# Denominators of phi for batches 0 and 1 from nine whole-array products of the exponentials, in a tile of their own

## The chip, the cores and the metric

The kernel runs on one core of a Trainium2 chip, in one launch. The metric is the device time of that launch in microseconds (us). A core has a matrix engine (TensorE, PE in the profile; its weight loads are listed apart as PEld), VectorE (DVE), ScalarE (ACT), GpSimd (POOL) and SyncE (SP), which here only issues DMAs. Each engine takes its instructions in order and waits for the others through semaphores. SBUF is the working memory of 128 partitions, PSUM the banks that TensorE writes to.

## The reference

Attention through 32 memories per head, then a gated feed-forward block with a product over the sequence (8 batches, 8 heads, 576 rows, 64 columns):

```
a = exp(phi - max(phi, over rows));  a = a / (sum(a, over rows) + 1e-9)
k_m = a^T k;  v_m = a^T v                              # 32 memories per head
attn = softmax(q k_m^T / 8);  x = attn v_m             # heads side by side: 576 x 512
h = relu(x w_in);  u, v = halves of h
v_n = (v - mean) / sqrt(var + 1e-6)
out = (u * (w_spatial v_n + b_spatial)) w_out
```

The change concerns `sum(a, over rows)`: one sum for each head and memory, 256 per batch.

## The kernel before, in words

Every batch goes through nine kinds of steps, each a generator that issues a few instructions and yields: P (`memory_weights`), K (`memories`), Q (`queries`), S (`scores`), M (`products`), V (`gate`), U (`units`), G (`spatial`), O (`project`). The weights have steps of their own: D, E and L load and decode w_in, X does w_out, W loads the spatial weights, T transposes them, B does the bias; Z is a warm-up product that nothing reads. Three written lists of letters say which step comes when: START (batch 0 from the beginning, batches 1 and 2 as far as they run ahead), PLAN (once per batch) and LAST. A quote mark means one batch ahead. Each engine's queue, SP's too, holds its instructions exactly in that order. The change does not touch the lists.

P loads the batch's phi into `phi_sb`, which has one buffer: 128 partitions are 2 heads x 64 groups of rows, and along a partition lie 4 head pairs j, 9 rows i of a group and 32 memories m. Step 1 issues the DMA (line 297). Steps 2 to 5 take the maximum over the 9 rows in four DVE operations (`over_rows`, lines 286 to 292), 6 to 9 take it across partitions (transpose, reduce, copy, transpose), 10 subtracts it on DVE (line 316), 11 is the exponential on ACT, in place (line 323), and 12 to 15 are the same four DVE operations with add: the sums over the 9 rows, tile `es`.

K loads k and v (steps 1 and 2). Steps 3 and 4 multiply the exponentials with k and v: 72 products in 64x32 pieces of the array (line 342; five values of i in step 3, four in step 4), and step 4 ends with eight small products that sum `es` over the 64 partitions of a head (line 354), into spare columns of the same two PSUM banks. Step 5 adds 1e-9 and takes the reciprocal on DVE (lines 364, 365: `den`). Steps 6 to 8 are copies on ACT that multiply by it (lines 369, 378), 9 and 10 transposes, 11 and 12 copies to `kT` and `vT`, from which S and M take their operands.

The part of START around the steps in question:

```
Q Z Q*3 Z P Q P*4 K Q P Q*2 P*2 K P Z P*6 K D1*2 K Z E0 K*3 D1 K Q*2 K D1 E1 E0 E1 P' Z K*2 W D0
...
V0 T1 P' L0 V2 V0 V2 L1 T3 T1 V0 P' V0 M0 B M0 P'*2 V0 V2 K' T1 M0*2 T4 K' P'' V0 K'*2 V0 T4 U2
```

So in batch 0 steps P 10 to 15 follow each other, and K 3 (the first of line 342) comes right behind. In batch 1 step P 12 stands between the first gate block's products (V0, line 621) and those of block V2, P 13 behind V0's statistics, P 14 and 15 behind M0's first step, and K 4 (second half of line 342 and line 354) two steps later. Batch 1's phi load (first P') is followed on SP's queue by W (spatial weights, lines 239 to 242) and D0 (w_in).

There is one pool of four single PSUM banks (`bank`) and one of two double ones (`banks`). A bank comes free when the last instruction that reads it is done. In START's last quoted line the two kvm banks of K', and one each for V0 and V2, are in use together; M0 takes two when they come free.

A float32 product appears in the trace as two weight loads and two matmuls.

Of the kernel before, what the change touches and what calls it, by code (L numbers as in the profile page):

```python
# [10 lines left out]
F32 = mybir.dt.float32  # L11
# [3 lines left out]
AF = mybir.ActivationFunctionType  # L15
ALU = mybir.AluOpType
# [39 lines left out]
def memory_attention_spatial_gate(  # L56
# [29 lines left out]
    nc = tc.nc  # L86
    B, H, S, D = q.shape
    MEM = phi.shape[3]
    DM = H * D
    DFF = w_in.shape[1]  # L90
    P = 128
# [3 lines left out]
    NJ = H // 2  # L95
    HALF = S // 2
    NB = S // 32
    NX = HALF // 32
    SCALE = 1.0 / math.sqrt(D)

    const = ctx.enter_context(tc.tile_pool(name="const", bufs=1))
    one = ctx.enter_context(tc.tile_pool(name="one", bufs=1))
# [5 lines left out]
    def bank(name):  # L108
        return ps1.tile([P, 512], F32, tag="b1", name=name)
# [11 lines left out]
    nc.scalar.activation(minus, ident, AF.Copy, scale=-1.0)  # L121

    phi_sb = const.tile([P, NJ, NX, MEM], F32, name="phi_sb")
    kv_sb = const.tile([P, NJ, 2, NX * D], F32, name="kv_sb")
    ones = const.tile([P, 2], F32, name="ones")
    nc.gpsimd.memset(ones, 1.0)
    t2 = const.tile([P, 512], F32R, name="t2")
    nc.gpsimd.memset(t2[SR:P, :].bitcast(F32), 1.0)

# [6 lines left out]
    state = {}  # L136
# [144 lines left out]
        yield  # L281


    def over_rows(to, op):
        half = one.tile([P, NJ, 4, MEM], F32, name="half")
        nc.vector.tensor_tensor(half, phi_sb[:, :, 0:4], phi_sb[:, :, 4:8], op=op)
        yield
        nc.vector.tensor_tensor(half[:, :, 0:2], half[:, :, 0:2], half[:, :, 2:4], op=op)
        yield
        nc.vector.tensor_tensor(to, half[:, :, 0], half[:, :, 1], op=op)  # L290
        yield
        nc.vector.tensor_tensor(to, to, phi_sb[:, :, 8], op=op)
        yield

    def memory_weights(b, _):

        nc.sync.dma_start(
            phi_sb.rearrange("p j i m -> p j (i m)"),
            phi[b].rearrange("(j r) (p i) m -> (r p) j (i m)", r=2, i=NX),
        )  # L300
        yield
        mx = one.tile([P, NJ, MEM], F32, name="mx")
        yield from over_rows(mx, ALU.max)
        mt = bank(f"mt_{b}")[:, 0:P]
        nc.tensor.transpose(mt, mx.rearrange("p j m -> p (j m)"), ident)
        yield
        cm = one.tile([P, 2], F32, name="cm")
        nc.vector.tensor_reduce(cm, mt.rearrange("s (r p) -> s r p", r=2), axis=AX.X, op=ALU.max)
        yield
        cmb = one.tile([P, 2, 64], F32, tag="vmn", name="cmb")  # L310
        nc.scalar.copy(cmb, cm[:, :, None].to_broadcast([P, 2, 64]))
        yield
        mb = bank(f"mb_{b}")[:, 0:P]
        nc.tensor.transpose(mb, cmb.rearrange("s r p -> s (r p)"), ident)
        yield
        nc.vector.tensor_tensor(
            phi_sb,
            phi_sb,
            mb.rearrange("p (j m) -> p j m", j=NJ)[:, :, None, :].to_broadcast([P, NJ, NX, MEM]),
            op=ALU.subtract,  # L320
        )
        yield
        nc.scalar.activation(phi_sb, phi_sb, AF.Exp)
        yield
        es = state["es", b] = one.tile([P, NJ, MEM], F32, tag="mx", name="es")
        yield from over_rows(es, ALU.add)

    def memories(b, _):
        for n, x in enumerate((k, v)):
            nc.sync.dma_start(  # L330
                kv_sb[:, :, n, :], x[b].rearrange("(j r) (p i) d -> (r p) j (i d)", r=2, i=NX)
            )
            yield

        kvb = [bank(f"kvm_{b}_{r}") for r in range(2)]
        kvm = [x[:, 0 : 2 * D].rearrange("p (n d) -> p n d", n=2) for x in kvb]
        esm = [x[:, 2 * D : 2 * D + 2] for x in kvb]
        halves = (slice(0, 64), slice(64, P))
        for i in range(NX):
            for j in range(NJ):  # L340
                for r in range(2):
                    nc.tensor.matmul(  # L342
                        kvm[r][32 * j : 32 * j + 32],
                        phi_sb[halves[r], j, i, :],
                        kv_sb[halves[r], j, :, i * D : (i + 1) * D],
                        start=(i == 0),
                        stop=(i == NX - 1),
                    )
            if i == 4:
                yield  # L350
        es = state.pop(("es", b))
        for j in range(NJ):
            for r in range(2):
                nc.tensor.matmul(
                    esm[r][32 * j : 32 * j + 32],
                    es[halves[r], j, :],
                    ones[halves[r]],
                    start=True,
                    stop=True,
                )  # L360
        yield
        den = one.tile([P, 2], F32, name="den")
        for r in range(2):
            nc.vector.tensor_scalar_add(den[:, r : r + 1], esm[r][:, 0:1], 1e-9)
        nc.vector.reciprocal(den, den)
        yield
        kmn = one.tile([P, 2, 2, D], F32, name="kmn")
        for r in range(2):
            nc.scalar.activation(
                kmn[:, r],  # L370
                kvm[r][:, 0, None, :].to_broadcast([P, 2, D]),
                AF.Copy,
                scale=den[:, r : r + 1],
            )
            yield
        vmn = one.tile([P, 2, D], F32, tag="vmn", name="vmn")
        for r in range(2):
            nc.scalar.activation(vmn[:, r], kvm[r][:, 1], AF.Copy, scale=den[:, r : r + 1])
        yield
        tk = bank(f"tk_{b}")[:, 0 : 2 * P]  # L380
        for r in range(2):
            nc.tensor.transpose(
                tk[:, r * P : (r + 1) * P], kmn[:, r].rearrange("p c d -> p (c d)"), ident
            )
        yield
        tv = bank(f"tv_{b}")[:, 0:P]
        nc.tensor.transpose(tv, vmn.rearrange("p r d -> p (r d)"), ident)
        yield
        kT = one.tile([P, 2, P], F32, name="kT")
        state["kT", b] = kT  # L390
        nc.scalar.copy(kT.rearrange("p r s -> p (r s)"), tk)
        yield
        vT = one.tile([P, P], F32, name="vT")
        state["vT", b] = vT
        nc.scalar.copy(vT, tv)
        yield
# [384 lines left out]
    def warm_up(b, _):  # L781
# [12 lines left out]
    }  # L794
    BATCH = {
        "P": memory_weights, "K": memories, "Q": queries, "S": scores, "M": products,
        "V": gate, "U": units, "G": spatial, "O": project,
    }
# [67 lines left out]
```

## Time and profile before

| | |
|---|---|
| median of 3 runs | 416.6 us (416.01 to 416.63) |
| the profiled execution | 417.52 us, of which the span from the first to the last instruction is 415.7 |
| ACT busy | 230.0 us (55%) |
| POOL busy | 46.5 us (11%) |
| weight loads (PEld) busy | 339.3 us (82%) |
| mean granted TensorE clock | 0.986 of full speed |
| DMA | 50.70 MB, mean 122 GB/s |

Busy time is the union of an engine's instructions. "Idle before, releaser" is the time that an engine stood before an instruction, and what ended it; "issue" means that the profile shows no reason. The chain of waits is followed back from the last instruction: at each step to what released it, or to the instruction before it on its engine. A granted clock of 1.00 is 2.4 GHz and 0.50 is 1.2 GHz.

### The profile page before, as it was taken

The numbers are of one execution on the slowest core, as the hardware profiler recorded it, in microseconds if no ns is written. First come the engines' busy times: TensorE is split into PE (matmuls) and PEld (weight loads), VectorE is DVE, ScalarE is ACT, GpSimd is POOL, SyncE is SP. The second block draws the span as 40 slices with busy tenths as digits, with TensorE's granted clock in tenths as the row PEclk, the third lists the DMA queues.
The fourth block names the chain that finished last, engine by engine and source line by source line (L and its number), as shares of the span: only waits on it lengthen the run. The fifth ranks groups of instructions, "written<-read, shape, count | busy, mean of one in ns | idle before, by whom it ended". The sixth has DMA issues, their size and how long they took to land.

```text
span 415.7 us, 9467 instructions
## 1 busy us (share of the span) xinstructions
PE 401.5 (97%) x3965; PEld 339.3 (82%) x3965; DVE 283.8 (68%) x540; ACT 230.0 (55%) x425; POOL 46.5 (11%) x131
## 2 busy tenths in 40 slices
PE   6789999999999999999999999999999999999996
PEld 3544788989798888978798888988798788989984
DVE  1477999986988468947888468947887368924430
ACT  2468889546644476337644476347734476348321
POOL 1000321003200210003200210003200210013000
PEclk9888999999999999999999999999999999999999
DMA  8899595035810891039500990049401510020003
GB/s 297 320 383 279 116 342 142 2 107 111 236 50 31 176 301 24 0 105 276 123 2 17 247 258 7 0 117 290 97 2 37 101 50 0 2 76 27 0 30 97
DMA packets 85790, 50.70 MB, mean 122 GB/s; under 512 B 66226, under 2 KB 70322, under 8 KB 85748
## 3 DMA queue, kind: packets, MB, share of 16 engines
q1 hardware_dynamic: 85748, 50.10, 42.0%
q8 instruction: 31, 0.51, 0.5%
q14 instruction: 11, 0.09, 0.1%
HBM read 40.65 MB, written 9.44 MB: 120 GB/s over the span
## 4 chain that ended last, share of the span: by engine, by line
PE 87%; DMA 4%; DVE 4%; ACT 3%; issue 1%; SPq 0%; ACTq 0%
PE ps L725 29%; PE po L765 22%; PE pu L687 12%; PE pv L621 10%; PE kvm L342 3%; PE mp L589 3%; PE sc L523 2%; DMA w_rem<-in_moe_w_spatial_dram 2%; DMA q_all<-in_q_dram 1%; PE idle L785 1%; PE pv L630 1%; PE pv L631 1%; DMA out_dram<-o 1%; PE tq L410 1%; PE wt L255 1%
## 5 line engine op out<-in xcount | busy, mean ns | idle before, releaser
L725 PE MATMUL ps<-wth,vh 128*128 128x288 f32 x256 | 57.1, 304 | 0.0
L725 PE MATMUL ps<-wth,vl 128*128 128x288 f32 x256 | 54.8, 296 | 0.0
L725 PE MATMUL ps<-wtl,vh 128*128 128x288 f32 x256 | 54.5, 294 | 0.0
L765 PE MATMUL po<-woh,gl 128*128 128x512 f32 x128 | 50.4, 394 | 0.0
L765 PE MATMUL po<-woh,gh 128*128 128x512 f32 x128 | 50.4, 394 | 0.0
L645 DVE BATCH_NORM_STATS2 st<-vr 128x6 f32<-128x512 f32 (+1 forms) x40 | 27.0, 675 | 34.1 <-ACT vr L626 33.3
L765 PE MATMUL po<-wol,gh 128*128 128x512 f32 x128 | 50.2, 392 | 0.0
L725 PEld LDWEIGHTS ps<-wth,vh 128*128 128x128 f32 x256 | 41.2, 190 | 8.7 <-ACT vh L663 5.0
L650 POOL TENSOR_SCALAR rs<-mv 128x1 f32<-128x1 f32 (+1 forms) x40 | 8.8, 221 | 330.4 <-DVE grl L749 153.4
L747 ACT CAST gh<-g 128x512 fp32r<-128x512 f32 x32 | 19.8, 621 | 46.4 <-DVE g L736 45.2
L771 ACT COPY o<-po 128x512 f32<-128x512 f32 x36 | 21.0, 584 | 37.3 <-PE po L765 20.0
L725 PEld LDWEIGHTS ps<-wth,vl 128*128 128x128 f32 x256 | 41.1, 188 | 0.0
L725 PEld LDWEIGHTS ps<-wtl,vh 128*128 128x128 f32 x256 | 41.1, 188 | 0.0
L736 DVE TENSOR_TENSOR g<-u,ps 128x576 f32<-128x576 f32 x32 | 23.4, 751 | 17.1 <-PE ps L725 17.1
L665 DVE TENSOR_TENSOR vl<-vr,vh 128x512 fp32r<-128x512 f32 x32 | 21.6, 681 | 18.0 <-ACT vh L663 17.8
L660 ACT ACTIVATE vr<-vr,sh,rs 128x512 f32<-128x512 f32 (+1 forms) x40 | 32.1, 816 | 3.0 <-POOL sh L655 3.0
L626 ACT ACTIVATE vr<-pv 128x512 f32<-128x512 f32 x32 | 19.2, 600 | 19.4 <-PE pv L621 13.1
L687 PE MATMUL pu<-ah,mh 128*128 128x288 f32 x128 | 28.7, 306 | 0.0
L765 PEld LDWEIGHTS po<-wol,gh 128*128 128x128 f32 x128 | 24.1, 188 | 5.2
L765 PEld LDWEIGHTS po<-woh,gl 128*128 128x128 f32 x128 | 24.1, 188 | 5.2
L765 PEld LDWEIGHTS po<-woh,gh 128*128 128x128 f32 x128 | 24.0, 188 | 5.2
L687 PE MATMUL pu<-al,mh 128*128 128x288 f32 x128 | 27.4, 296 | 0.0
(141 smaller groups left out, 861.3 us busy)
## 6 DMA issues: line engine op xcount, KB each, us to landing
kv_sb<-in_k_dram SPq DMA_DIRECT2D x8, 1152.0 KB, 7.0
kv_sb<-in_v_dram SPq DMA_DIRECT2D x8, 1152.0 KB, 7.7
out_dram<-o SPq DMA_DIRECT2D x32, 256.0 KB, 2.3
q_sb<-in_q_dram SPq DMA_DIRECT2D x28, 288.0 KB, 5.6
phi_sb<-in_phi_dram SPq DMA_DIRECT2D x8, 576.0 KB, 5.0
raw<-in_moe_w_in_dram SPq DMA_DIRECT2D x8, 512.0 KB, 10.3
raw<-in_moe_w_out_dram SPq DMA_DIRECT2D x4, 512.0 KB, 6.0
q_all<-in_q_dram SPq DMA_DIRECT2D x1, 1152.0 KB, 5.4
```

Source lines behind the costliest of these rows:

```text
L342: nc.tensor.matmul(kvm[r][32 * j : 32 * j + 32], phi_sb[halves[r], j, i, :], kv_sb[halves[r], j, :, i * D : (i + 1) * D], start=(i == 0), ...
L621: nc.tensor.matmul(pv, x[:, r, cs], m[:, r, DM:DFF], start=(n == 0), stop=(n == 5))
L626: nc.scalar.activation(vr, pv, AF.Relu)
L645: nc.vector.bn_stats(st6, vr)
L660: nc.scalar.activation(vr, vr, AF.Identity, bias=sh, scale=rs)
L665: nc.vector.tensor_tensor(vl[:, st, :], vr, vh[:, st, :].bitcast(F32), op=ALU.subtract)
L687: nc.tensor.matmul(pu[:, hf, 0:HALF], m[:, r, cs], a[:, r, hf * HALF : (hf + 1) * HALF], start=(n == 0), stop=(n == 5),)
L725: nc.tensor.matmul(ps[:, hf, 0:HALF], a, w[:, hf * HALF : (hf + 1) * HALF], start=(n == 0), stop=(n == len(ops) - 1),)
L736: nc.vector.tensor_tensor(g.rearrange("p (a s) -> p a s", a=2), u[:, dt, :].rearrange("p (a s) -> p a s", a=2), ps[:, :, 0:HALF], op=ALU.mult,
L747: nc.scalar.copy(hi, x)
L765: nc.tensor.matmul(po, a, w, start=(n == 0), stop=(n == 11))
L771: nc.scalar.copy(o, po)
```

## The change

The exponentials get a tile of their own, `phi_exp`, with rows ahead of head pairs, so that for one row i the 4 x 32 columns (j, m) lie together. For batches 0 and 1 step P 12 issues nine products, one for each i: the 128x128 block of exponentials is the stationary operand, and `side`, two columns that mark the partitions of either head, moves. They accumulate in a bank of their own and give all 256 sums. P 13 adds 1e-9 and takes the reciprocal; P 14 and 15 are empty. In K the eight small products and the denominator's operations are left out for these batches. Batches 2 to 7 keep both, reading from `phi_exp`.

```
+    phi_exp = const.tile([P, NX, NJ, MEM], F32, name="phi_exp")
...
+    side = const.tile([P, 2], F32, name="side")
+    nc.gpsimd.memset(side, 0.0)
+    for r in range(2):
+        nc.gpsimd.memset(side[64 * r : 64 * r + 64, r : r + 1], 1.0)
...
-    def over_rows(to, op):
+    def over_rows(to, x, op):
...
-        nc.scalar.activation(phi_sb, phi_sb, AF.Exp)
-        yield
+        nc.scalar.activation(phi_exp.rearrange("p i j m -> p j i m"), phi_sb, AF.Exp)
+        yield
+        if b < 2:
+            sums = bank(f"es_{b}")[:, 0:2]
+            for i in range(NX):
+                nc.tensor.matmul(
+                    sums, phi_exp[:, i].rearrange("p j m -> p (j m)"), side, start=(i == 0), stop=(i == NX - 1)
+                )
+            yield
+            den = state["den", b] = one.tile([P, 2], F32, name=f"den_{b}")
+            nc.vector.tensor_scalar_add(den, sums, 1e-9)
+            nc.vector.reciprocal(den, den)
+            yield
+            return
         es = state["es", b] = one.tile([P, NJ, MEM], F32, tag="mx", name="es")
-        yield from over_rows(es, ALU.add)
+        yield from over_rows(es, phi_exp.rearrange("p i j m -> p j i m"), ALU.add)
...
                         kvm[r][32 * j : 32 * j + 32],
-                        phi_sb[halves[r], j, i, :],
+                        phi_exp[halves[r], i, j, :],
...
-        es = state.pop(("es", b))
-        for j in range(NJ):
+        if b < 2:
+            yield
+            den = state["den", b]
+        else:
+            es = state.pop(("es", b))
+            for j in range(NJ):
...
             for r in range(2):
-                nc.tensor.matmul(
...
-        yield
-        den = one.tile([P, 2], F32, name="den")
-        for r in range(2):
-            nc.vector.tensor_scalar_add(den[:, r : r + 1], esm[r][:, 0:1], 1e-9)
-        nc.vector.reciprocal(den, den)
+                nc.vector.tensor_scalar_add(den[:, r : r + 1], esm[r][:, 0:1], 1e-9)
+            nc.vector.reciprocal(den, den)
         yield
```

## Rows read from the trace of the kernel before

**Rows 1.** The page's first part: busy us, share of the span, instructions.

```profile
PE 401.5 (97%) x3965; PEld 339.3 (82%) x3965; DVE 283.8 (68%) x540; ACT 230.0 (55%) x425; POOL 46.5 (11%) x131
```

**Rows 2.** Chain of waits, 0 to 60 us: start us, us, what.

```profile
18.58 0.38 SPq L297
...
19.81 6.77 DMA w_rem<-in_moe_w_spatial_dram
...
26.63 0.64 PE wt L255 x3
27.27 1.57 issue
...
29.83 2.00 PE idle L785 x2
...
48.52 0.27 PE kvm L354 x13
```

**Rows 3.** Instructions in order of time, 0 to 25 us: start, us, instruction, idle before.

```profile
14.55 0.69 DVE L286 TENSOR_TENSOR half<-phi_sb 128x512 f32<-128x512 f32 x1 [1.23 <-ACT phi_sb L323]
...
14.57 3.87 PE L342 MATMUL kvm<-kv_sb,phi_sb 64*32 64x128 f32 x144 [1.78 <-ACT phi_sb L323]
...
19.20 0.63 ACT L369 ACTIVATE kmn<-kvm,den 128x128 f32<-128x128 f32 x2 [1.63 <-DVE den L365]
...
22.05 2.52 PE L454 MATMUL sc<-kT,qT_all 64*64 64x32 f32 x144
```

**Rows 4.** Busy by stretch: us, then PE PEld DVE ACT POOL, PEclk, DMA share, GB/s.

```profile
14.75:15.00 0.25, 0.25 (x24) 0.25 (x17) 0.25 (x1) 0.00 (x0) 0.00 (x0) 0.62 1.07 426
...
18.25:18.50 0.25, 0.25 (x29) 0.23 (x12) 0.00 (x0) 0.00 (x0) 0.00 (x0) 1.00 0.32 82
...
18.00:20.00 2.00, 1.53 (x41) 0.68 (x23) 1.28 (x4) 0.80 (x4) 0.00 (x0) 0.94 0.27 56
...
28.25:28.50 0.25, 0.00 (x0) 0.00 (x0) 0.25 (x1) 0.00 (x0) 0.00 (x0) 0.93 1.07 426
...
30.00:32.00 2.00, 2.00 (x4) 0.97 (x5) 0.94 (x1) 1.03 (x2) 0.00 (x0) 0.50 1.03 401
```

**Rows 5.** Groups by form: weight loads at 36 to 41 us, matmuls over the run.

```profile
L785 PEld LDWEIGHTS idle<-ident 128*128 128x128 f32 x2 | 0.3, 190 | 0.0
...
L354 PE MATMUL kvm<-ones,es 64*32 64x2 f32 x128 | 2.4, 169 | 0.1
```

**Rows 6.** Chain of waits over the whole run.

```profile
49.23 1.13 PE wt L255 x10
...
64.44 8.45 PE ps L725 x62
...
92.04 2.08 PE kvm L342 x138
```

**Rows 7.** Instructions in order of time, 40 to 60 us.

```profile
42.96 0.67 DVE L286 TENSOR_TENSOR half<-phi_sb 128x512 f32<-128x512 f32 x1
...
44.88 0.62 ACT L626 ACTIVATE vr<-pv 128x512 f32<-128x512 f32 x1
...
45.28 0.40 PE L621 MATMUL pv<-mh,al 128*128 128x512 f32 x1
...
45.71 0.60 ACT L626 ACTIVATE vr<-pv 128x512 f32<-128x512 f32 x1 [0.21 <-PE pv L621]
...
47.25 1.14 PE L342 MATMUL kvm<-kv_sb,phi_sb 64*32 64x128 f32 x60
...
48.18 0.29 DVE L292 TENSOR_TENSOR es<-es,phi_sb 128x128 f32<-128x128 f32 x1
```

**Rows 8.** PE's weight loads that waited: us in total, times, longest.

```profile
PEld mp L589 <- ACT vr L626: 1.0, 2, 0.6
...
PEld pv L621 <- ACT o L771: 1.8, 2, 1.1
```

More of the change, by code (lines that the diff above doesn't have):

```diff
@@ L281, in prepare_bias @@
         yield
-    def over_rows(to, op):
+    def over_rows(to, x, op):
         half = one.tile([P, NJ, 4, MEM], F32, name="half")
-        nc.vector.tensor_tensor(half, phi_sb[:, :, 0:4], phi_sb[:, :, 4:8], op=op)
+        nc.vector.tensor_tensor(half, x[:, :, 0:4], x[:, :, 4:8], op=op)
         yield
@@ L291, in over_rows @@
         yield
-        nc.vector.tensor_tensor(to, to, phi_sb[:, :, 8], op=op)
+        nc.vector.tensor_tensor(to, to, x[:, :, 8], op=op)
         yield
@@ L302, in memory_weights @@
         mx = one.tile([P, NJ, MEM], F32, name="mx")
-        yield from over_rows(mx, ALU.max)
+        yield from over_rows(mx, phi_sb, ALU.max)
         mt = bank(f"mt_{b}")[:, 0:P]
@@ L350, in memories @@
                 yield
-        es = state.pop(("es", b))
-        for j in range(NJ):
-            for r in range(2):
-                nc.tensor.matmul(
[L355 to L360, printed above, removed]
-        yield
-        den = one.tile([P, 2], F32, name="den")
-        for r in range(2):
-            nc.vector.tensor_scalar_add(den[:, r : r + 1], esm[r][:, 0:1], 1e-9)
-        nc.vector.reciprocal(den, den)
+        if b < 2:
[4 more added lines that the diff above has]
+            for j in range(NJ):
+                for r in range(2):
+                    nc.tensor.matmul(
+                        esm[r][32 * j : 32 * j + 32],
+                        es[halves[r], j, :],
+                        ones[halves[r]],
+                        start=True,
+                        stop=True,
+                    )
+            yield
+            den = one.tile([P, 2], F32, name="den")
+            for r in range(2):
+                nc.vector.tensor_scalar_add(den[:, r : r + 1], esm[r][:, 0:1], 1e-9)
+            nc.vector.reciprocal(den, den)
         yield
```

## The prediction

> **What bounds the kernel now.** I read the busy times first: TensorE (PE) 97%, VectorE (DVE) 68% [rows 1]. Those are averages over two very different stretches, so I went to the chain of work that ended last. There the reader sees two regimes. Up to 48.5 us the end is handed from engine to engine: batch 0's phi load waits at the head of SP's queue until 18.58, the spatial weight's last rows (w_rem) land at 26.6, PE then stands for 1.57 us, runs a warm-up at half speed, and after a run of ScalarE (ACT) and DVE work the last add of batch 1's sums releases PE at 48.52 [rows 2]. From there on the chain is PE, product after product [rows 2, 6]. So what an edit does before 48.5 us counts only through the next thing that PE, or ACT's run, waits for; a microsecond that it adds to PE's own stream later counts in full, since nothing later waits long enough to swallow it.
>
> **What is removed and added, per early batch.** Removed: four DVE adds, first 0.67, last 0.29 us [rows 7] (by the chain 0.4 and 0.3 between), some 1.6 us; the three small denominator steps become two and move ahead; and the eight small products of line 354, which the trace shows as 16 instructions in 0.27 us [rows 2], go too. Added: nine products with a whole 128x128 block of exponentials as weights and two columns moving. The eight products of line 354 appear as 16 loads and matmuls, so nine are 18 weight loads and 18 matmuls.
>
> Their price is not in the trace. From below: if a pair went at the pace of line 354, 0.27/16 = 17 ns, 18 cost 0.3 us. From above: if no load overlapped anything, 190 ns of load and 169 ns of a two-column matmul [rows 5] make 18 x 0.36 = 6.5 us. Nearest are streams in which each product has its own 128-column weights: ten transposes in 1.13 us, 113 ns each, and 62 spatial products in 8.45 us, 136 ns each with 288 columns moving [rows 6]. Line 354 is farther off, because its loads are 32 columns wide and spread over eight pieces of the array. I take 115 ns: 18 x 0.115 = 2.1 us at full clock.
>
> A rule speaks against the change here. The trace shows a 128-column load at 190 ns [rows 5]. The Trainium skill, page "TensorE: Matmul & The Clock Gate", section "LDWEIGHTS (loading the stationary operand)", says that a load is paid by its columns and not by its rows, columns over 1.2 in ns. By that estimate 18 loads of 128 columns are 18 x 107 ns = 1.9 us however few columns move, and the forecast would come out 0.2 us lower per batch; the trace agrees in size, since 113 ns is its densest pace.
>
> **Batch 0.** The products go where the exponentials end, 14.57 us. PE has then waited 1.78 us [rows 3], and the granted clock falls to 0.50 (1.2 GHz) within the first 0.3 us and is back at 1.00 only near 18.2 [rows 4]. At half clock the 144 instructions of line 342 took 3.87 us [rows 3], against 2.08 later for 138 [rows 6], a factor near 1.8. So the nine products take 0.3 us plus 15.5 pairs x 0.115 x 1.8 = 3.2, together 3.5 us, to 18.1. Then line 342 runs at full clock, 2.2 us, to 20.3. The denominators are ready by then (their two short DVE steps have 2 us of cover), so the scaled copies start at 20.3 instead of 19.20 [rows 3]: +1.1 us. The 1.6 us of adds that leave DVE at 14.55 gain nothing; they ran beside line 342.
>
> The separate tile moves the next load as well. Batch 1's phi load waited for the last reader of phi_sb; now only the exponential reads it, so it issues near 14.6 instead of 18.58, and the spatial weights behind it on SP's queue, the four decode loads and the next k and v with it. The DMA engines were full to 18 us and idle for most of 18 to 20 [rows 4], so what is behind moves some 1.5 to 2 us, not 4: w_rem lands near 25. But PE comes later: the score products, 22.05 to 24.57 before [rows 3], end at 25.7, a warm-up of 1.0 follows, and seven spatial transposes of 0.2 each (as the last three took, 26.63 to 27.27) end near 28.1, where 27.27 was. The early load buys back only 0.3 us of the 1.1. The 1.57 us stand and the half clock after it [rows 2, 4] I leave as they are: **+0.8 us** on the ACT run that starts from these transposes. From below, with the clock not falling there, this is -0.7; from above, with the clock not coming back at 18.2, +2.5 (both are rivals).
>
> **Batch 1.** The clock is full. The products sit between the first and the third gate block's products (lines 621), so the latter end at 45.28 + 0.23 + 2.1 = 47.6 instead of 45.5; ACT's copy out of that bank started at 45.71 on it [rows 7], and the two win_sb products wait for the bank. All of that moves by 2.1. Line 342's second half ended at 48.39 [rows 7]; the 0.13 us to 48.52 and line 354's 0.27 go away: 2.1 - 0.4 = **+1.7 us** for PE's stream. The new bank makes four of four in use, so the later gate block must wait for the first one's copy, which ends at 44.88 + 0.62 = 45.5 [rows 7], 0.5 us before PE is through with the nine products: nothing; if it gets the new bank instead, freed after DVE's next step, +0.6. DVE's 1.6 us there is real, but PE itself is busy to 48.39, so it gives 0.13.
>
> **The rest**, at nothing: three more memsets on POOL lie beside the first loads; the exponentials' write in another order and the adds of batches 2 to 7 from it have the same elements, and DVE has a third of its time free. Batches 2 to 7 load phi up to 2 us earlier, beside output stores; the only wait there that such a collision could lengthen cost PE's loads 1.8 us in two places [rows 8], PE itself less, so 1 us either way.
>
> **Sum.** 0.8 + 1.7 = +2.5 us. The profiled execution took 417.52 (span 415.7 and 1.8 around it), so 420.0 for its like; it stands 0.9 above the median of the runs, 416.6, on which the forecast is made: 419.1.
>
> **Rivals.**
> 1. The clock costs more: at 18.2 it does not return, since before its rise there PE ran line 342's products and now other work stands in their place; line 342 then runs at half, 3.9 us, the copies start 2.8 late and 2.5 of it arrives. For it: PE was also busy from 28.8 to 31.8 and the clock stayed at 0.50 [rows 2, 4]. Against: line 342 follows at once. Likewise the nine products of batch 1 may let it fall, some 1.7 us. Either gives about 420.8.
> 2. The clock does not fall at 28.4, as PE is now busy later and has less waiting before it. The 3.0 us from 28.84 to 31.83 (the warm-up alone is 2.0 of them [rows 2]) would take half: 419.1 - 1.5 = 417.6. Against: the 1.57 us stand remains.
> 3. Faster: DVE, not PE, is the bound up to 48.5, and the products go into PE's waits. The chain names DVE's adds as what ended last before 48.52 [rows 2]. Then batch 1 gains the 1.6 us of adds instead of losing 1.7, and with batch 0's +0.8 it is 415.8. It decides if a load and matmul pair goes below some 22 ns (0.4 us saved over 18), or if PE has 1.7 us of wait between 41 and 48. Against: the waits there are 1.0 us [rows 8], behind ACT copies that themselves wait for the shifted products.
>
> **Chances.** Forecast 0.40, rival 1 0.25, rival 2 0.18, rival 3 0.17. A change of under 0.2% (0.8 us) cannot be told from none. Rival 2 lies beside that bound and is halved: slower 0.74, same 0.09, faster 0.17. The range leaves a tenth out on each side: into rival 3 below, 415.8, and past rival 1 above, 421.2. The likeliest case's own range is 418.2 to 420.2.
>
> **What would show it.** Right: 18 loads of a new line before line 342 in batches 0 and 1, near 2.1 us in batch 1 and 3.5 in batch 0; scaled copies near 20.3; SP's second phi load near 14.6; w_rem near 25; line 342's second half of batch 1 ending near 50.9. Wrong: pairs well under 50 ns; a granted clock of 1.00 from 28 to 35; PE idle for over 1.5 us around the new products of batch 1; a growing wait for output copies after 125 us.

## The result, and the profile after

The changed kernel takes 423.0 us (median of 6 runs, 421.4 to 427.9), the kernel before 416.6 us in the same job: a ratio of 1.0137, 95% interval 1.0108 to 1.0166, so 5.7 us slower [4.5 to 6.9]. One of the six runs, 427.9, lies over 1.5% above the fastest and is left out of the ratio and of every mean, median and count below; the other five have a median of 421.9. Forecast was 2.5 us slower, 419.1, and not above 421.2. The direction held and the size didn't. The profiled execution of after took 421.69 us (span 419.6, 2.1 around it, granted clock 0.992), that of before 417.52 (0.986). The two profiles thus lie 4.2 us apart, the medians 5.3.

Busy us, share of the span and instructions of each engine of the kernel after; before: [rows 1].

```profile
PE 403.9 (96%) x3969; PEld 341.3 (81%) x3969; DVE 280.8 (67%) x530; ACT 230.2 (55%) x425; POOL 47.7 (11%) x134
```

PE has 2.4 us more, DVE 3.0 less, ACT the same: the work went to the engine that was the bound.

Batch 0 in after, in order of time; before: [rows 3].

```profile
14.57 0.38 SPq L302 DMA_DIRECT2D phi_sb<-in_phi_dram  x1
...
14.69 2.14 PE L333 MATMUL es<-side,phi_exp 128*128 128x2 f32 x18 [1.87 <-ACT phi_exp L328]
...
16.77 3.69 PE L359 MATMUL kvm<-kv_sb,phi_exp 64*32 64x128 f32 x144
...
20.46 0.63 ACT L390 ACTIVATE kmn<-kvm,den 128x128 f32<-128x128 f32 x2 [2.73 <-PE kvm L359]
...
23.32 2.56 PE L475 MATMUL sc<-kT,qT_all 64*64 64x32 f32 x144
```

Busy by stretch in after: us, PE, PEld, DVE, ACT, POOL, granted clock, DMA share, GB/s; before: [rows 4].

```profile
14.69:16.80 2.11, 2.11 (x24) 2.09 (x26) 0.00 (x0) 0.23 (x1) 0.00 (x0) 1.00 1.02 406
17.40:20.80 3.40, 3.40 (x118) 3.01 (x101) 1.23 (x1) 0.67 (x3) 0.00 (x0) 0.50 1.05 374
...
28.40:31.00 2.60, 1.02 (x6) 0.79 (x7) 2.60 (x3) 0.61 (x2) 0.00 (x0) 1.00 1.02 399
31.00:34.40 3.40, 3.40 (x18) 1.45 (x21) 2.52 (x6) 2.30 (x4) 0.00 (x0) 0.50 1.06 393
```

The reader is to see that the nine products ran at full clock, in 2.14 us, and that the clock then went to 0.50 (1.2 GHz), 0.5 us behind them, so that the 144 products of line 359 took 3.69 us. I had it the other way round, 3.5 and 2.2. The copies start at 20.46 either way. The second half-clock stretch begins at 31.0, where it began near 28.5 before.

The chain of waits of after, 20 to 53 us: start us, us, what; before: [rows 2, 6].

```profile
28.32 0.70 DVE sm_all L491
29.02 0.96 issue
29.98 0.86 PE wt L260 x5
...
43.51 1.68 PE pv L642 x6
45.20 1.90 PE es L333 x18
47.10 1.49 PE pv L642 x6
...
51.30 0.43 PE mp L161
51.73 1.14 PE wt L260 x10
```

In the chain of before the product that is line 161 here (line 156 there), behind the second half of line 342, stood at 48.80:

```profile
48.80 0.44 PE mp L156
```

Here it starts at 51.30: 2.5 us later, the sum of the forecast to the tenth. Then more is lost.

60 to 73 us in order of time, first before, then after.

```profile
64.34 0.77 POOL L655 TENSOR_SCALAR sh<-mv,rs 64x1 f32<-64x1 f32 x1
64.39 0.68 DVE L665 TENSOR_TENSOR vl<-vr,vh 128x512 fp32r<-128x512 f32 x1
64.99 1.34 DVE L543 TENSOR_TENSOR sm<-sm,rmx 128x1152 f32<-128x1152 f32 x1
65.45 0.83 ACT L660 ACTIVATE vr<-vr,sh,rs 64x512 f32<-64x512 f32 x1
```

```profile
66.85 2.04 POOL L676 TENSOR_SCALAR sh<-mv,rs 64x1 f32<-64x1 f32 x1
66.89 0.68 DVE L686 TENSOR_TENSOR vl<-vr,vh 128x512 fp32r<-128x512 f32 x1
67.49 1.34 DVE L564 TENSOR_TENSOR sm<-sm,rmx 128x1152 f32<-128x1152 f32 x1
68.92 0.82 ACT L681 ACTIVATE vr<-vr,sh,rs 64x512 f32<-64x512 f32 x1 [0.87 <-POOL sh L676]
...
72.67 0.53 PE L746 MATMUL ps<-ws,t 128*128 128x288 f32 x2 [0.51 <-ACT t L692]
```

`sh`, a product of 64 numbers that the change doesn't touch (the last gate block's normalization in batch 0), took 2.04 us where it had taken 0.77. It ends 0.06 us behind DVE's subtraction; in before it ended 0.04 behind the operation ahead of that one. ACT and at last PE wait for it, and PE's step from batch 2's first phi transposes to its second ones (steps 6 and 9 of P, tiles `mt` and `mb`; the expectations below call batch 2's mt#3 and mb#3) grew from 12.01 to 12.74 us: the shift there is 3.2. Another 0.6 comes behind 76 us, and the span ends 3.9 late.

### The profile page after: what moved, and what is told of

Same layout as the page of the kernel before. It is cut to its first block, busy times and chain, and to the rows that moved or that the text cites. A ratio compares the mean times of both kernels' runs of the same rounds, so it can differ in the third digit from the quotient of the medians.

```text
span 419.6 us, 9470 instructions
## 1 busy us (share of the span) xinstructions
PE 403.9 (96%) x3969; PEld 341.3 (81%) x3969; DVE 280.8 (67%) x530; ACT 230.2 (55%) x425; POOL 47.7 (11%) x134
## 4 chain that ended last, share of the span: by engine, by line
PE 86%; DVE 4%; ACT 4%; DMA 3%; issue 1%; POOL 1%; ACTq 0%
PE ps L746 28%; PE po L786 20%; PE pu L708 11%; PE pv L642 10%; PE kvm L359 4%; PE mp L610 3%; PE sc L544 2%; DMA out_dram<-o 2%; PE idle L806 2%; DMA q_all<-in_q_dram 1%; PE es L333 1%; DVE phi_sb L321 1%; PE pv L652 1%; PE pv L651 1%; ACT phi_exp L328 1%
## 5 line engine op out<-in xcount | busy, mean ns | idle before, releaser
L757 DVE TENSOR_TENSOR g<-u,ps 128x576 f32<-128x576 f32 x32 | 23.4, 750 | 16.7 <-PE ps L746 16.7
L647 ACT ACTIVATE vr<-pv 128x512 f32<-128x512 f32 x32 | 19.2, 601 | 22.0 <-PE pv L642 21.9
```

The costliest lines, as they stand in the source:

```text
L647: nc.scalar.activation(vr, pv, AF.Relu)
L757: nc.vector.tensor_tensor(g.rearrange("p (a s) -> p a s", a=2), u[:, dt, :].rearrange("p (a s) -> p a s", a=2), ps[:, :, 0:HALF], op=ALU.mult,
```

## The experiments

All runs are of kernels that differ from before or after in the edit named, and nothing is left out of the computation. A ratio is that to the kernel before in the same job. "Mean" is over all executions of a kernel; a standard error stands behind it in brackets.

| kernel | executions | median us | ratio, 95% interval | granted clock of its executions |
|---|---|---|---|---|
| before, the four later jobs | 80 | 417.4 | | 0.982 to 1.000 |
| after, two jobs | 11 | 422.3 | 1.0108 to 1.0166, 1.0106 to 1.0175 | 0.982 to 0.992 |
| tile_alone | 12 | 417.35 | 0.9993 to 1.0034 | 0.991 to 1.000 |
| batch0_alone | 6 | 420.14 | 1.0059 to 1.0126 | 0.986 to 0.992 |
| batch1_alone | 6 | 420.94 | 1.0070 to 1.0139 | 0.984 to 1.000 |
| batch1_double | 4 | 424.44 | 1.0114 to 1.0203 | 0.984 to 0.996 |
| wide_products | 6 | 422.49 | 1.0070 to 1.0144 | 0.992 to 0.996 |
| after_warm | 6 | 422.37 | 1.0082 to 1.0160 | 0.988 to 0.992 |
| before_warm | 12 | 417.65 | 0.9969 to 1.0022 | 0.988 to 1.000 |
| idle_tile | 12 | 417.54 | 0.9976 to 1.0022 | 0.986 to 1.000 |
| tile_held | 12 | 417.37 | 0.9998 to 1.0037 | 0.987 to 1.000 |
| before_sh_dve | 12 | 417.95 | 0.9981 to 1.0026 | 0.984 to 1.000 |
| after_sh_dve | 6 | 422.24 | 1.0094 to 1.0162 | 0.984 to 0.992 |
| wide_sh_dve | 6 | 423.40 | 1.0100 to 1.0161 | 0.982 to 0.996 |
| before_sh_act | 12 | 416.98 | 0.9977 to 1.0021 | 0.982 to 0.996 |
| after_sh_act | 6 | 422.72 | 1.0089 to 1.0159 | 0.986 to 0.992 |

### Which part costs: the tile, batch 0, batch 1

```
-        if b < 2:          # both places
+        if b < 0:          # tile_alone
+        if b < 1:          # batch0_alone
+        if b == 1:         # batch1_alone
```

> Only the tile of their own for the exponentials; the denominators of all batches are made as before. Theory (TensorE's own stream pays, the tile is nearly free): within 0.5 us of before, with the second phi load issued near 14.6 us instead of 18.58. Rival (the earlier loads collide with instruction loads or output stores): at least 1.5 us slower, with longer stands of TensorE between 25 and 30 us or behind output copies.

> The nine products in batch 0 alone, with the tile. Theory: the scaled copies start 1.1 to 1.3 us late and 0.8 to 1.3 us of it reach the end. Rival (late work later on, not the products' own time, makes the loss): under 0.5 us, since it needs both batches' delays.

> The nine products in batch 1 alone, with the tile. Theory: the second half of line 359's products ends 1.6 to 1.8 us late, and that reaches the end: 1.5 to 2.2 us slower. Rival (late work later on): over 3 us, with a stand of TensorE or a slow GpSimd instruction between 60 and 76 us.

> The changed kernel again. Theory: the sum of the two single batches within 0.7 us. Rival (the granted clock decides): single executions fall into groups 2 to 3 us apart, each group with its own mean granted clock, and the kernel before has such groups too.

The means are 417.6 (tile), 420.7 (batch 0) and 421.4 (batch 1) against 417.5 for before: the tile 0.1 (0.3), as its theory had it, batch 0's products 3.1 over it (0.5), batch 1's 3.8 over it (0.6). Each alone costs more than the whole forecast, so the theories of both runs missed, and so did batch 0's rival. Batch 1's rival has its time, over 3 us, but not its reason: `sh` took the 2.03 us that it takes in most kernels here. Together they cost 5.3 over the tile (0.5), 1.6 less than the two alone (0.9): the theory of after_again missed. Its rival came true in part: after's eleven executions stand at 421.4 to 422.3 with a clock of 0.992, and at 423.1 to 425.3 with 0.982 to 0.988. Batch 0 and 1 alone, busy by stretch, columns as above:

```profile
14.50:16.60 2.10, 2.10 (x23) 2.08 (x24) 0.00 (x0) 0.07 (x1) 0.00 (x0) 1.00 1.02 408
16.60:20.25 3.65, 3.65 (x146) 3.27 (x145) 1.55 (x3) 1.10 (x1) 0.00 (x0) 0.56 1.05 384
```

```profile
43.50:45.00 1.50, 1.50 (x8) 1.22 (x8) 1.40 (x5) 0.00 (x0) 0.44 (x2) 0.65 0.76 91
45.00:47.25 2.25, 2.25 (x13) 0.93 (x19) 0.51 (x2) 0.81 (x2) 1.03 (x2) 0.50 1.00 363
```

The products of batch 0 end at 16.6 and those of batch 1 (in batch1_alone) at 43.8, and a stretch at 0.50 begins within 0.4 us of the end of either, though PE isn't without work for a moment. In the profiles that have both (after, after_again, after_warm, after_sh_dve, after_sh_act) the clock is 1.00 from 43 to 52 us: batch 1's products bring a fall only where batch 0's have brought none. PE's stream shows what that is worth: from batch 1's second phi transposes to batch 2's first it takes 23.3 to 23.4 us in the eight profiles without batch 1's products, 25.0 to 25.1 in the five with both, and 26.2 in batch1_alone. So 1.2 us of batch 1's cost is absent where batch 0's products ran. That is of the size of the 1.6 us by which the parts don't add up, which the times alone don't set clear of noise.

### Is it the products or the wait ahead of them that lowers the clock?

```
wide_products:                                # same sums, 128 columns move
-            sums = bank(f"es_{b}")[:, 0:2]
+            wide = bank(f"es_{b}")[:, 0:P].rearrange("p (r c) -> p r c", r=2)
+            cols = side[:, :, None].to_broadcast([P, 2, 64])
...
-                    sums, phi_exp[:, i]..., side, ...
+                    wide, phi_exp[:, i]..., cols, ...
+            sums = wide[:, :, 0]
after_warm, before_warm:                      # one warm-up more in the wait
-    ... P*2 K P Z P*6 K D1*2 ...
+    ... P*2 K P Z*2 P*6 K D1*2 ...
```

> The changed kernel, but each of the nine products moves 128 columns (the two marker columns 64 times over) instead of two. The sums are the same. Theory (the weight loads set the pace, and the clock falls because so little moves in the products): the products take no more than 2.4 us in batch 1, as the 128 columns pass under the next load; the granted clock does not fall behind batch 0's products, and the whole is 1 to 2 us faster than the changed kernel. Rival (the clock falls because of the wait ahead of the products): the same half-clock stretch from about 17 to 20.8 us, and the time of the changed kernel or up to 1 us more.

> The changed kernel with one more warm-up product in TensorE's wait for batch 0's exponentials, where it fits (1.0 us of 1.87). Theory (little moves in the products): the clock still falls behind them in most executions, time within 0.7 us of the changed kernel. Rival (the wait ahead of them): the stretch from 17 to 20.8 us is gone in most executions, line 359 in batch 0 takes 2.2 instead of 3.6 us, and the whole is 1 to 1.5 us faster.

> The kernel before with the same warm-up product. Theory (its half-clock stretch behind 14.6 us, present in some executions only, comes from the wait): that stretch is gone from all executions, and the median falls by 0.3 to 1 us. Rival (that stretch has nothing to do with the wait): same as before, within 0.3 us.

PE of after_warm and of wide_products in order of time, and the same of before_sh_dve, which is the kernel before up to here:

```profile
14.89 2.14 PE L333 MATMUL es<-side,phi_exp 128*128 128x2 f32 x18 [0.97 <-issue]
16.96 3.32 PE L359 MATMUL kvm<-kv_sb,phi_exp 64*32 64x128 f32 x144
```

```profile
14.99 2.25 PE L334 MATMUL es<-side,phi_exp 128*128 128x128 f32 x18 [1.76 <-ACT phi_exp L328]
17.16 2.25 PE L361 MATMUL kvm<-kv_sb,phi_exp 64*32 64x128 f32 x144
19.45 0.62 ACT L392 ACTIVATE kmn<-kvm,den 128x128 f32<-128x128 f32 x2 [1.71 <-PE kvm L361]
```

```profile
14.43 2.25 PE L342 MATMUL kvm<-kv_sb,phi_sb 64*32 64x128 f32 x144 [1.78 <-ACT phi_sb L323]
17.44 0.60 ACT L369 ACTIVATE kmn<-kvm,den 128x128 f32<-128x128 f32 x2
```

With the wait cut to half by a warm-up, line 359 still took 3.32 us: the length of the wait isn't what lowers the clock behind the products, as far as one profile shows. No run had the products without any wait. The same warm-up in before gains nothing that can be measured (0.9969 to 1.0022), so the rival was right there. With 128 columns moving, line 361 ran at full clock. In all six profiles with two-column products in batch 0 (after, after_again, batch0_alone, after_warm, after_sh_dve, after_sh_act) the products run at 1.00 and what follows at half; wide_sh_dve, the second profile with wide products, shows another pattern, the one of before's profile: the clock fell during them.

```profile
15.08 3.67 PE L334 MATMUL es<-side,phi_exp 128*128 128x128 f32 x18 [1.87 <-ACT phi_exp L328]
18.68 2.41 PE L361 MATMUL kvm<-kv_sb,phi_exp 64*32 64x128 f32 x144
```

So wide products don't hold the clock up in every execution: one profile of two. The executions agree: all 35 with two-column products in batch 0 have a granted clock of at most 0.992, of before's 80 only 40, of the 12 with wide products 6. Nor did they win time: the forecasts of 1 to 2 us, and of 420.5 to 421 for wide_sh_dve, missed (means 422.6 and 422.8, after 422.8).

The rows of before_sh_dve are the ones that matter. Nine profiles have the old batch 0 up to the copies (before, idle_tile, before_sh_dve, before_sh_act, before_warm, tile_alone, tile_held, batch1_alone, batch1_double). In seven line 342 takes 2.2 us and the copies start at 17.4 to 17.7; only in before's own and in idle_tile's it takes 3.8 and they start at 19.1 to 19.2. The one profile that I had was of the rarer kind.

The price of the stretch at the end isn't settled by wide_products, though: its copies came 1.0 us earlier, batch 2's first transposes 0.9, and PE's step from there to the second ones took 3.3 more than in after. In that step `sh` took 3.86 us, PE stood for 1.07 and 0.94 us, and then the clock fell again, with PE busy throughout at half speed:

```profile
73.50:77.20 3.70, 3.65 (x16) 3.65 (x17) 2.95 (x4) 3.70 (x5) 0.00 (x0) 0.54 0.00 0
```

The time is within the spread of after's.

### What one pair costs

```
-            for i in range(NX):
+            for n in range(2 * NX):        # and b == 1 only: every product twice
+                i = n % NX
```

> The nine products of batch 1 issued twice (the second pass starts the sums again), batch 0 as before, with the tile. Theory (their own time on TensorE is what reaches the end): 2.0 to 2.2 us slower than with one pass, so about 422.9. Rival (most of the loss is their place: the bank, the copies behind it, the clock): under 1 us or over 3 us more than one pass.

18 more pairs took 2.0 us more (36 in 4.08 us against 18 in 2.07), and batch 2's first phi transposes came 2.3 us later, as the theory has it. The mean rose by 3.1 us (0.9), 424.4 against 421.4 of batch1_alone, which would be the rival's side but is too wide to decide. A pair with two columns moving costs 113 to 119 ns in every profile here at full clock, a whole-array load each, as forecast (115). The rest of the 3.1 isn't taken apart; the clock is at 0.50 behind the doubled products as well.

```profile
47.25:49.00 1.75, 1.75 (x11) 0.46 (x17) 0.48 (x2) 1.11 (x2) 0.00 (x0) 0.50 1.07 415
```

### The tile by itself

```
idle_tile (on before):
+    pad = const.tile([P, NX, NJ, MEM], F32, name="pad")
+    nc.gpsimd.memset(pad[:, 0, 0, 0:2], 0.0)
tile_held (on tile_alone):
             nc.vector.reciprocal(den, den)
+            nc.vector.memset(phi_sb[:, 0, 0, 0:1], 0.0)
```

> The kernel before with one more tile of the size of phi_exp, of which only a memset of two columns is ever written and which nothing reads; no order, load or product differs. What is asked: of the 1.1 us (at full clock) that the own tile alone cost, 0.3 lie outside the profiled span. If the place that the tile takes in memory costs that (allocation, launch), this kernel shows it too: 0.3 over before outside the span, 416.9. If the cost is what the tile lets happen (earlier loads of phi, exponentials and adds in another layout), this kernel is at 416.6 with 1.8 outside the span, as before.

> The kernel with the own tile alone (no product of the change in any batch), and one DVE memset of phi_sb's first column behind each batch's reciprocal, so that the next batch's phi load has to wait for it as it waited for the last small product before. Output is the same. Asked: the own tile alone cost 0.9 us at full clock, of which 0.3 outside the span, and an idle tile cost nothing. If the earlier loads cost it (collisions with output stores), this kernel falls back to 416.1 at full clock; if the layout of the exponentials and the adds or the start of the program cost it, it stays at 417.0.

The place in memory costs nothing that can be measured (idle_tile 0.9976 to 1.0022, 1.8 us outside the span). With the phi loads held back (17.64 us in tile_held, 13.77 in tile_alone) the mean is 417.8, without 417.6: by raw times the early loads neither cost nor gain anything that can be measured, and the tile costs 0.1 to 0.3 us. At full clock, as the expectation counts, the model in the section on why the prediction failed has tile_held at 416.4 and tile_alone at 417.0, which would put the cost on the loads. The two disagree, so whether the loads cost anything stays open. What every kernel with the tile in use shows is 0.2 to 0.3 us outside the span: 2.1 where before has 1.8 (1.95 to 2.01 where `sh` is moved as well). Where that comes from stays open; it isn't allocation.

### The 0.7 us between 60 and 73

```
             sh = two.tile([P, 1], F32, name="sh")[0:rows]
-            nc.gpsimd.tensor_scalar(sh, mv[:, 0:1], rs, -1.0, ...)
+            (nc.vector if b == 0 and st == NI else nc.gpsimd).tensor_scalar(...)   # _sh_dve
+            if b == 0 and st == NI:                                                # _sh_act
+                nc.scalar.activation(sh, mv[:, 0:1], AF.Identity, scale=-1.0)
+                nc.scalar.activation(sh, sh, AF.Identity, scale=rs)
```

> The kernel before, but the small product sh of batch 0's last gate block (64x1) is computed on DVE instead of POOL. Theory: on POOL it runs against DVE's two long operations and takes 0.77, 2.04 or 3.86 us as it falls; on DVE it takes under 0.15 us, waits for POOL's rs some 0.6 to 0.9 us at most, and the ACT activation behind it is never late. In before's profile it had been let through at 0.77, so most executions of before would gain 0.3 to 0.7: 416.1. Rival: the wait in DVE's order costs what POOL's wait cost, since the exponentials' subtraction behind it is late instead: 416.6 or more.

> The changed kernel with the same edit (sh of batch 0's last gate block on DVE). Theory: the 0.73 us that PE's stream loses between 60.7 and 72.7 us goes; mt#3 stays 2.5 late, mb#3 is 2.5 late instead of 3.2, and the time is 422.0 where the changed kernel has 422.7. Rival: the 0.73 us is PE's own stream (the earlier loads of phi, or another product order), and it stays: 422.7.

> The changed kernel with products that move 128 columns each, and sh of batch 0's last gate block on DVE. Theory: the wide products keep the granted clock at 1.00 behind batch 0's exponentials, which is worth 1.5 us of the spell of 17.0 to 20.5 in the changed kernel, and the gain was hidden in the earlier run by sh at 3.86 us; with sh on DVE the time is 420.5 to 421. Rival: the two-column products' low clock is given back elsewhere in any case (one spell more or less in the first 50 us of every execution), and it stays at 422.

> The kernel before, with sh of batch 0's last gate block on ACT in two small steps (the negated mean, then times rs) instead of POOL. On DVE it had to wait behind the 1.34 us subtraction in DVE's order, and PE lost the same 0.8 us as with POOL shut out. ACT stands for 0.87 us there, so theory: PE's step from batch 2's first transposes to its second ones takes 12.0 us, as in the one profile of before in which POOL got through, and 0.7 less than with the slow sh; 417.0 where before has 417.6 in the mean. Rival: the wait is then on POOL's rs, itself held up, and nothing changes.

> The changed kernel with the same edit. Theory: batch 2's second transposes stand as late against before's profile as its first ones (2.0 to 2.5 us), where they had 0.73 more; the time is 422.5 where the changed kernel has 423.2 in the mean. Rival: the 0.73 us is something else, and stays.

On DVE nothing was won; the rival was right. before_sh_dve in order of time:

```profile
63.69 1.34 DVE L543 TENSOR_TENSOR sm<-sm,rmx 128x1152 f32<-128x1152 f32 x1
64.96 0.20 DVE L655 TENSOR_SCALAR sh<-mv,rs 64x1 f32<-64x1 f32 x1
...
65.19 0.82 ACT L662 ACTIVATE vr<-vr,sh,rs 64x512 f32<-64x512 f32 x1 [0.92 <-DVE sh L655]
```

In DVE's order `sh` stands behind the same subtraction that shuts POOL out, so ACT waits 0.92 us, and PE's step from batch 2's first to its second transposes is 12.81 us; in after_sh_dve it is 12.80, and in idle_tile, which has `sh` on POOL at 2.03 us, 12.73. On ACT, which isn't behind DVE, `sh` is ready in time, after_sh_act:

```profile
66.18 0.29 ACT L678 ACTIVATE sh<-sh,rs 64x1 f32<-64x1 f32 x1 [0.19 <-POOL rs L672]
...
66.89 1.34 DVE L564 TENSOR_TENSOR sm<-sm,rmx 128x1152 f32<-128x1152 f32 x1
...
67.92 0.82 ACT L685 ACTIVATE vr<-vr,sh,rs 64x512 f32<-64x512 f32 x1
```

The step falls to 12.33 us (12.38 in before_sh_act): some half of the 0.73. The other half goes to ACT itself: the two small steps and the wait for rs push its queue back, and the activation starts 2.34 us after the second step of rs began (65.58), in before 1.76 (63.69), in after 2.73 (66.19). The times say nothing either way: the means, 422.1 against 422.8 and 417.1 against 417.5, point down by 0.7 (0.8) and 0.3 (0.3). Moving `sh` therefore shows that the wait is real and the same in before; it is no explanation of the difference between the kernels. Of twelve profiles with `sh` on POOL ten have it at 2.03 or 2.04 us and one at 3.86; before's 0.77 was the exception.

No kernel here beats the kernel before.

## Why the prediction failed

The mechanism held. The products go to the engine that is the bound, at 115 ns a pair. (The lower bound of that price misread its row: the 0.27 us hold 13 instructions there and not 16; nothing hangs on it.) Against before's own profile PE's stream is 0.81 us late at batch 1's second phi transposes (forecast +0.8) and 1.7 more at 57 us (forecast +1.7). The lines of before, of tile_alone, of batch0_alone and of after:

```profile
37.39 0.27 PE L314 MATMUL mb<-ident,cmb 128*128 128x128 f32 x1
36.04 0.28 PE L319 MATMUL mb<-ident,cmb 128*128 128x128 f32 x1
38.16 0.30 PE L319 MATMUL mb<-ident,cmb 128*128 128x128 f32 x1
38.20 0.30 PE L319 MATMUL mb<-ident,cmb 128*128 128x128 f32 x1
```

The 1.7 holds in every profile with both batches' products: 25.0 to 25.1 us of PE's stream where the others take 23.3 to 23.4. The 0.81 is luck, as the next paragraph shows. Rival 3, that DVE is the bound, is refuted: batch1_alone isn't faster but 3.9 us slower than before in the mean, and PE is busy without a gap around the products. "The rest, at nothing" held within 0.3 us.

The step that failed is the term for batch 0, "+0.8 us": the scaled copies were to start "at 20.3 instead of 19.20 [rows 3]: +1.1 us", and most executions don't start them at 19.20. The profiled execution ran line 342 at half clock, 3.87 us; in seven of the nine profiles with the old batch 0 it takes 2.2, and the copies start at 17.4 to 17.7. Against that start batch 0's products move the copies to 20.4, by 2.9 us and not by 1.1. Of these 2.9, 2.1 arrive: batch 1's second transposes are 2.1 us later in batch0_alone than in tile_alone, and the spans differ by 2.2; in the means 3.1 (0.5). That is the term of 0.8, mis-sized by 1.3 to 2.3 us.

The profile of before was no expensive one for all that. At batch 1's second transposes it is 1.1 to 1.8 us behind the six other profiles that have neither batch's products (37.39 against 35.64 to 36.33), but its span, 415.7, lies among theirs, 415.4 to 416.4. Its quick `sh` gives back 0.7, and at 213 us it is 0.2 behind their mean. So the sentence that nothing behind 48.5 us swallows a delay doesn't hold for this one; what swallowed the rest of it isn't found. And 417.52 was an ordinary time: the 80 later executions of before have a median of 417.4, so there was little ground for the 0.9 between the profile and the runs. That moves the forecast's time and not its difference.

Within batch 0, "the nine products take 0.3 us plus 15.5 pairs x 0.115 x 1.8" and "line 342 runs at full clock" were both wrong, in opposite directions: 2.14 and 3.69 us, 5.8 together where I had 5.7. The agreement of 20.46 with 20.3 is two errors that cancel. This is rival 1 in its place, not in its reason: the clock didn't stay low because other work stood before its rise, it fell behind the products. For batch 1, where the rival names the products as the cause, it came true in batch1_alone, 3.8 us over the tile in the mean, but not in after's profile: there the clock stayed at 1.00 and the term of 1.7 was exact.

Rival 2 came partly true, in the profile of after: the clock at 28.4 was still 1.00 and fell at 31.0, for 3.4 us where before's profile had 6.8.

The traces don't show the whole difference. The five profiles of after (two) and its three variants with the same products have spans of 419.0 to 419.7 us, 3.5 over the mean of the seven with neither batch's products, and 0.3 lie outside: 3.8. The means over all executions differ by 5.4 (0.4). Some of what is missing lies in executions without a trace: of the 29 of after and these variants 14 have a granted clock of at most 0.988 and take 423.7 in the mean, the other 15 take 421.6; of before's 80 only 14 are as low (419.2, the others 417.1). Where the clock fell in them nothing kept can show.

To see how much is clock and how much is work I fitted one time for every kernel and one common slope to all executions above: time against (1 - granted clock) x span. It gives 0.51 (standard error 0.03) us per us, and at a clock of 1.00: before 416.0, tile_alone 417.0, batch0_alone 418.4, batch1_alone 419.5, after 420.5 (0.1 to 0.4 each). By it after is 4.5 us of work and 0.8 of clock; the parts give 4.9 of work, 1.0 (tile), 1.4 and 2.5 (batches). This is a model and no measurement: the slope is a mean over stretches that cost differently, the tile's 1.0 comes from its executions having a higher clock without being faster, and the wide products, with a higher clock, weren't faster for it.

Two smaller steps missed. The early load bought nothing visible: w_rem, issued at 15.55 where it was 19.81, landed 10.7 us later, not 6.8, near 26.3 (forecast 25), while the DMA engines were full (share 1.05 at 17.4 to 20.8) where before had a gap. And PE's stand was 2.41 us instead of the 1.57 that I left "as they are":

```profile
PE wt L260 <- DVE sm_all L491: 2.4, 1, 2.4
```

The release named is doubtful: DVE's sm_all ended at 29.02 and PE started at 29.98. The stand comes two pairs of instructions earlier in PE's order than before, which is what batch 0 gained (36 for 32); in batch1_double, with batch 0 as before, it stands where it stood. That fits PE's own instructions arriving late from memory (`issue` in the chain), and the traces bear it out: a 16 KB transfer on the queue that brings instructions ends at 28.50 in after and at 27.44 in before, and PE starts 1.48 and 1.40 us behind it. In 16 of the 17 profiles the 706th record of PE and PEld, counted together, starts 1.3 to 1.5 us behind the end of that transfer, whatever product stands there; no run moved the transfer by itself.

So by the traces the sum should have been 2.1 for batch 0, 1.7 for batch 1 and 0.3 outside the span, 4.1; with the 3.1 that the means give batch 0, and the tile's 0.1, it is 4.9, inside the 4.5 to 6.9 measured. What stays open: what the 0.3 us outside the span is, how much of batch 0's 2.1 to 3.1 the low clock behind its products is, where the executions with the lowest clock lose their time, and why batch 1's products lower the clock only where batch 0's didn't.

## What to carry to other kernels

Before a cost is worked out from one profile, ask whether the stretch that it starts from is typical: where the clock fell in that execution is part of its time, and an edit that brings such a stretch into every profile must be priced against the executions without it. On a kernel bound by PE, sums moved from VectorE to PE cost what the weight loads cost, some 115 ns for each 128x128 block, however few columns move, and what follows them may run at half clock. A tiny operation that another engine waits for is not cheap when it stands behind, or beside, a long operation of DVE.

## What the runs showed of the hardware

- Eighteen pairs of a whole-array weight load and a two-column matmul ran in 2.06 to 2.14 us at a granted clock of 1.00. In batch 0, where PE had stood for 1.87 us (0.97 in after_warm) ahead of them, the clock went to 0.50 within 1.0 us of their end in six profiles of six, for some 3.4 us, with PE busy all the time (2.11 of 2.11 us while they ran). Behind batch 1's it did so in two profiles of seven, with 18 pairs and with 36.
- POOL's product of 64 numbers took 0.77, 2.04 or 3.86 us as DVE's operations beside it followed each other. The last, in wide_products, ended only when DVE stood still, behind four operations in a row:

```profile
65.95 3.86 POOL L678 TENSOR_SCALAR sh<-mv,rs 64x1 f32<-64x1 f32 x1
65.99 0.68 DVE L688 TENSOR_TENSOR vl<-vr,vh 128x512 fp32r<-128x512 f32 x1
66.59 1.34 DVE L566 TENSOR_TENSOR sm<-sm,rmx 128x1152 f32<-128x1152 f32 x1
67.86 1.21 DVE L194 SCALAR_TENSOR_TENSOR raw<-raw 128x1024 int32<-128x1024 int32 x1
69.00 0.68 DVE L688 TENSOR_TENSOR vl<-vr,vh 128x512 fp32r<-128x512 f32 x1
```

The Trainium skill, page "SBUF — State Buffer", section "Who interferes with whom", says that a DVE instruction with two inputs in SBUF contends with a GpSimd instruction that reads SBUF, since its second input comes through the read interface that the two share, that such a shared port is held as an exclusive lock, and that the order of issue decides who waits. The ends 0.04 and 0.06 us behind a DVE operation with two inputs agree, so does `sh` on ACT, which doesn't wait. That POOL loses though its record starts 0.04 us ahead of DVE's, and to several DVE operations in a row, is this trace's.

- The granted clock of single executions of one kernel went from 0.982 to 1.000 in the kernel before, with times from 415.0 to 420.1 us. One execution doesn't show where it falls in the next.
